# A long-convolution and maxout kernel: the passage from the last frequency pairs to the first feed-forward, with its order, its PSUM banks and its first load changed

## The chip, the cores and the metric

The kernel runs on one core of a Trainium2 chip. The metric is the device time of one execution in microseconds (us); "before" is the median of three runs, and a profile comes from one further execution. Engines are named as in the profile: PE is TensorE's matmul (PEld its weight load), DVE is VectorE, ACT is ScalarE, POOL is GpSimd, SP is SyncE, which only issues DMAs here. Times inside a trace are microseconds from the start of its span.

## The reference: what is computed

Four sequences of 12,544 positions and 128 channels pass a causal long convolution with one learned filter, are multiplied by `x`, and go through a maxout feed-forward with three weight matrices:

```
h = maximum(pos_emb @ w1, 0) @ w2 * exp(-0.01 * pos)        # the filter
u = x * v
y = irfft(rfft(u, 2S) * rfft(h, 2S))[:S];   a = x * y
out = maximum(maximum(a @ moe_w1, a @ moe_w2), a @ moe_w3) @ moe_w_out
```

All of it is float32.

## The kernel before

**The convolution** is a transform of 128 times 90 points with shifted frequencies, split into four stages of matmuls. The first stage turns the 98 samples of each residue into 90 frequencies and keeps them in `spec` (the signal) and `specH` (the filter). The 90 frequencies then go as 45 pairs g (NK = 45) through the second stage (`g_second`, `butterfly`), the product with the filter's spectrum (`g_swap`, `g_re`, `g_im`), the inverse butterfly (`g_unfold`, which makes `ab`) and the third stage (`g_third`, line 649), whose result `zs` is copied by ACT and stored by SP to the DRAM tensor `zd[0]`: one store of two rows for each pair. The fourth stage works on tiles (b, i) of 4 positions times 98 samples: `t_load` (776) reads `zt`, the rows of all 45 pairs for both parts c of a complex number; `t_sums` (799) makes a sum and a difference; `t_last` (815) multiplies by the table `f4p` and then by `x` (`xT`, from `x_load`, 769) into `gt`.

**The feed-forward** uses max(a,b,c) @ wo = max(b-a, c-a, 0) @ wo + a @ wo. `up` (834) makes 128 of the 768 hidden rows: two products into two of the three PSUM banks `hps`, a Relu on ACT (839), a maximum on DVE (842). `down` (845) multiplies by `moe_w_out`. The product `lin` = moe_w1 @ moe_w_out is needed first; it is made by six **folds** (`fold`, 1097): PE transposes 128 columns of moe_w1 (`pt`, 1099), ACT copies them (`w1t`, 1101), PE multiplies them and adds into the bank `pl`. `folding` (1166) lets the multiplication of a fold follow two folds later.

**The order of the work** is written out by hand: every engine executes its own instructions in the order in which the code issues them, and semaphores order the engines among each other. In steps s = 0 to 47 (line 1174) step s issues the second stage of pair s, the filter spectrum of pair s-1 (`s_filter`, into the double bank `h`, copied by ACT to `ht`), the third stage of pair s-3, and the products of pair s-2. The filter spectra are also stored for the later batches (`s_store`, on POOL's queue, ahead of the products). In step 45 two pairs, 43 and 44, are multiplied. Line 1196 says on which engine the addition of `g_im` is done: POOL for 1 < s < 44, DVE otherwise.

Beside these steps the first stage of batch 1 is prepared: `u_load`, `u_mul` (DVE), `u_turn` (a transposition on PE, two copies on ACT) and the **units**, `u_first` (488), which are 32 small matmuls into two banks, a copy on ACT (`high`, 461) and eight operations on DVE: four "sums" (471) and four "fours" (482, 485) that write into `spec`.

After the second stage of pair 44 the order before is: filter 44, third stage 42, unit 0 (step 45); third stage 43, folds 0 to 2 (step 46); third stage 44 (step 47); unit 1, fold 3, turn 4, fold 4, turn 5, fold 5. The order after that is the same in both kernels: units 2, 3 and 4 with their DVE work, the first tile's sums and fourth stage, and the first `up`.

**PSUM.** In this stage the eight banks belong to the pools `cps` (tag `cv`, three banks, used by the second and third stages and by the folds), `sps` (`h`, a double bank, and `pl`) and `gps` (`g`, two banks). A tile asked of a tag takes the next of its buffers and waits until that buffer's last reader is done.

**Queues of DMAs.** SP carries the z stores, the third stage's weights (`load_dir`, 972), `u_load`, and most loads; POOL carries the filter stores and `xT`. For the first tile SP loads `zt` of part 0 and POOL that of part 1; both come after the store of pair 44. The tile (0, 1) is loaded by SP right after it, and (0, 2) in the first `up` (1277), together with its `xT` on POOL.

Of the kernel before, what the change touches and what calls it, by code (L numbers as in the profile page):

```python
# [10 lines left out]
FP32 = mybir.dt.float32  # L11
# [5 lines left out]
P = 128  # L17
# [78 lines left out]
def kernel(  # L96
# [15 lines left out]
    nc = tc.nc  # L112
# [4 lines left out]
    NF = DFF // P  # L117
    NK = N1 // 2
# [9 lines left out]

    zd = [dram.tile([N1, 2, 64, 256] if b == 0 else [N1, 2, 32, 2, 256], FP32, name=f"zd{b}")
          for b in range(B)]  # L130

    f1_t, f1e_t, f1h_t, f4p_t, w_t, wq_t = tables(NB)
    f1_d = nc.inline_tensor(f1_t, name="f1_const").ap()
# [354 lines left out]
    def u_first(*args):  # L488
        for fn in u_products(*args):
            fn()  # L490
# [144 lines left out]
    def g_im(g, apart=False):  # L635
        xt, xs = xts[g], xss.pop(g)
        nc.vector.tensor_tensor(out=xs[:], in0=xs[:], in1=hts.pop(g)[1][:], op=ALU.mult)
        (nc.gpsimd if apart else nc.vector).tensor_tensor(
            out=xt[:], in0=xt[:], in1=xs[:], op=ALU.add)

    def g_unfold(g):
        y = xts.pop(g)
        ab = state["cv"][0].tile([P, 2, 2, D], FP32, tag="ab", name="ab", bufs=2)
        for q, op in enumerate((ALU.add, ALU.subtract)):
            nc.vector.tensor_tensor(out=ab[:, :, q, :], in0=y[:, :, 0, :], in1=y[:, :, 1, :],
                                    op=op)
        abs_[g] = ab

    def g_third(g):
        w, ab = ws.pop((g, 1)), abs_.pop(g)  # L650
        ps = state["cv"][1].tile([P, 512], FP32, tag="cv", name="ps3")
        for k in range(2):
            for q in range(2):
                halves_mm(ps[:, (2 * k + q) * D:(2 * k + q + 1) * D], w[:, k, q, :],
                          ab[:, k, q, :], k == 0 and q == 0, True)
        if g < NK - 2:
            zs = state["cv"][0].tile([P, 2, 256], FP32, tag="z", name="zs", bufs=2)
        else:
            zs = lwp.tile([P, 2, 256], FP32, tag="w1", name="zs")
        nc.scalar.copy(zs[:].rearrange("p k f -> p (k f)"), ps[:])  # L660
        nc.sync.dma_start(
            zd[0][2 * g:2 * g + 2].rearrange("k c t f -> (c t) k f"), zs[:])

# [103 lines left out]
    zts, xTs, gs, pos_, obs = ({} for _ in range(5))  # L767
# [5 lines left out]
                          x[:, 4 * i:4 * i + 8, c, b, :])  # L773
        xTs[b, i], xTs[b, i + 1] = xT[:, 0], xT[:, 1]

    def t_load(b, i, queues=(nc.sync, nc.sync)):
        if b == i == 0:
            x_load(b, i, nc.gpsimd)
        zt = hp.tile([N1, 2, 512], FP32, tag="zt", name="zt", bufs=2)
        for c in range(2):  # L780
            if b == 0:
                queues[c].dma_start(
                    zt[NK * c:NK * c + NK],
                    zd[b].rearrange("(g a) c t f -> g a c t f", a=2)[
                        :, :, c, 2 * i:2 * i + 2, :].rearrange("g a t f -> g a (t f)"))
                continue
            q, j = divmod(i, NT // 2)
            for a in range(2):
                nc.sync.dma_start(
                    zt[NK * c:NK * c + NK, a].rearrange("g (t f) -> g t f", t=2),  # L790
                    zd[b].rearrange("(g a) c t q f -> g a c t q f", a=2)[
                        :, a, c ^ (a & q), 2 * j:2 * j + 2, q, :])
        zts[b, i] = zt[:, 0], zt[:, 1]
        if i % 2 == 0 and (b, i) not in xTs:
            x_load(b, i, nc.gpsimd if 0 < i < NT - 2 and b < B - 1 else nc.sync)

    evens_ = {}
# [282 lines left out]
    cps = pro.enter_context(tc.tile_pool(name="cps0", bufs=3, space=PSUM))  # L1080
    sps = pro.enter_context(tc.tile_pool(name="sps", bufs=1, space=PSUM))
    gps = pro.enter_context(tc.tile_pool(name="gps", bufs=2, space=PSUM))
    def banks_of():
        for pool, tag, n in ((gps, "g", 1), (gps, "g", 1), (sps, "h", 2), (gps, "g", 1),
                             (cps, "cv", 1), (gps, "g", 1)):
            yield pool.tile([P, 512 * n], FP32, tag=tag, name="ps1")[:, 0:512]

    free = banks_of()

    def bank():  # L1090
        return next(free)

    state = {"cv": (cvp, cps), "xb": 2, "bank": bank, "wide": ("ht", 2),
             "turn": lambda: sps.tile([P, 512], FP32, tag="pl", name="pst")}
    Gs, lows = {}, {}

    def fold(f):
        pt = cps.tile([P, 512], FP32, tag="cv", name="pt")
        nc.tensor.transpose(pt[:, 0:D], w_sb[0][:, f * P:(f + 1) * P], eye[:])
        w1t = cvp.tile([P, 2, D], FP32, tag="G", name="w1t", bufs=2)  # L1100
        nc.scalar.copy(w1t[:, 0], pt[:, 0:D])
        return lambda: halves_mm(pl[:, 0:D], w1t[:, 0], wo_sb[:, f, :], f == 0, f == NF - 1)
# [63 lines left out]
    def folding(f):  # L1166
        folded.append(fold(f))
        if len(folded) > 2:
            folded.pop(0)()

    def unit(u):
        u_first(u, (bank(), bank()), "x")

    for s in range(NK + 3):
        if s < NK:
            ws[s, 0] = wf[s]
            s_second(s)
            g_second(s)
            wf.pop(s)
            if s + 3 < NK:  # L1180
                wf[s + 3] = load_dir(s + 3, 0)
        if 1 <= s <= NK:
            g_swap(s - 1)
            s_filter(s - 1)
        if s >= 3:
            ws[s - 3, 1] = wi.pop(s - 3)
            g_third(s - 3)
            if s < NK:
                wi[s] = load_dir(s, 1)
        ready = [g for g in {NK: (s - 2, s - 1)}.get(s, (s - 2,)) if 0 <= g and s <= NK]  # L1190
        for g in {NK - 2: (s - 2, s - 1), NK - 1: (s - 1,), NK: (s - 1,)}.get(s, (s - 2,)):
            if 0 <= g and s <= NK:
                s_store(g)
        for g in ready:
            g_re(g)
            g_im(g, 1 < s < NK - 1)
        if s < NK:
            s_sums(s)
            g_butterfly(s)
        for g in ready:  # L1200
            g_unfold(g)

        if s in muls:
            u_mul(muls[s])
        if s in turns:
            u_turn(turns[s])
        if s in loads:
            u_load(1, loads[s])
        if s == NK:
            unit(0)  # L1210
            pl = sps.tile([P, 512], FP32, tag="pl", name="pl")
        if s == NK + 1:
            for f in range(3):
                folding(f)
    unit(1)
    state["turn"] = bank
    for f in range(3, NF):
        folding(f)
        if f in (3, 4):
            u_turn(f + 1)  # L1220
    while folded:
        folded.pop(0)()
    nc.scalar.copy(lin[:], pl[:, 0:D])
# [5 lines left out]
    f4p = hp.tile([N1, 2, 2, NB // 2], FP32, name="f4p", bufs=1)  # L1229
    nc.sync.dma_start(f4p[:], f4p_d)  # L1230
    sign_t = hp.tile([N1, 1], FP32, name="sign", bufs=1)
    nc.sync.dma_start(sign_t[:], sign_d)
    op_ = ctx.enter_context(tc.tile_pool(name="op", bufs=2))
    conv = ExitStack()
    wp = conv.enter_context(tc.tile_pool(name="wp", bufs=3))
# [19 lines left out]
    for n, (b, i) in enumerate(tiles[:LAST]):  # L1255
        if i == 0:
            plan, pairs_from = plans[b]
        if n == 0:
            t_load(*tiles[0], (nc.sync, nc.gpsimd))
            t_load(*tiles[1])  # L1260
            second_ = u_products(2, (next(hbanks), next(hbanks)))
            second_[0]()
            first_ = ops.tile([D, 512], FP32, tag="ops", name="ps1")
            spare = state["bank"]()
            third = u_products(3)
            fourth = u_products(4, (spare[:, 0:512], spare[:, 512:1024]), "xs")
            t_sums(tiles[0], nc.vector)
            third[0]()
            second_[1]()
            fourth[0]()  # L1270
            t_last(tiles[0], first_)
            second_[2]()
            for fn in fourth[1:]:
                fn()
        for f in range(NF):

            if i < NT - 2:
                if f == 0:
                    t_load(*tiles[n + 2])
            elif i == NT - 1 and f < 2 and n + 1 + f < len(tiles):  # L1280
                t_load(*tiles[n + 1 + f])
            turn_ = i == NT - 1
            if f == 4 and n + 1 == LAST:
                t_sums(tiles[n + 2], nc.vector)
            h = up((b, i), f)
            if n == 0 and f in (1, 2):
                third[f]()
            for a in range(2):
                if f == plan[i][a]:
                    t_sums(tiles[n + 1],  # L1290
                           nc.vector if turn_ or i * NF > pairs_from else nc.gpsimd, (a,))
            late.append(((b, i), f, h))
            if len(late) > 2:
                down(*late.pop(0))
            if f == plan[i][2]:
                t_last(tiles[n + 1])
            if f == 5 and n + 1 == LAST:
                t_last(tiles[n + 2])
            run(besides.pop(n * NF + f, ()))
# [100 lines left out]
```

## Time and the profile before

| | |
|---|---|
| median of 3 runs | 2213.24 us (2212.88 to 2213.73) |
| the profiled execution | 2213.66 us, its span 2211.9 us |
| PE busy | 2192.4 us, 99% of the span |
| DVE, ACT, POOL busy | 69%, 55%, 54% |
| chain that ended last | PE 96%, DMA 1%, DVE 1%, issue 1%, ACT 1% |
| mean granted TensorE clock | 0.997 |
| third stage of pair 44, its copy on ACT ends | 279.1 us, 280.9 us |
| first feed-forward matmul | 292.4 us |

How to read it. A profile counts an engine as busy while one of its instructions runs. "Idle before, releaser" is the time for which the engine had nothing to run before an instruction, and what its wait ended on. The chain of waits goes back from the last instruction, at each step to what released it; so only work that is named there can shorten the time. The view by stretches cuts the span at given times and shows each engine's busy time and the mean granted clock in each.

The passage that the change touches lies between about 255 and 300 us of the span: from the last pairs' products to the first feed-forward.

### The profile page before, as it was taken

To read this page: it belongs to the slowest core of one execution; us is meant where nothing else is said; L and a number is where in the kernel's file an instruction comes from. 1 tells how busy PE (TensorE), PEld (TensorE's weight loads), DVE (VectorE), ACT (ScalarE), POOL (GpSimd) and SP (SyncE) were. 2 spreads that over 40 slices of the span, in tenths; PEclk is the share of its full clock that TensorE was granted. 3 is DMA by queue.
4 is the path that set the end of the run, shared out by engine and by line. 5 is a ranking of instruction groups with operands and counts; after the bars stand their busy time and mean duration, and the time that the engine had idled before them with its cause. 6 is when DMAs were issued, how large, how long until landed. Compare 5 with 4: busy or idle time off the path is not lost.

```text
span 2211.9 us, 77196 instructions
## 1 busy us (share of the span) xinstructions
PE 2192.4 (99%) x31655; PEld 1288.0 (58%) x31655; DVE 1532.6 (69%) x3291; ACT 1211.3 (55%) x2223; POOL 1183.9 (54%) x1579
## 2 busy tenths in 40 slices
PE   9999999999999999999999999999999999999999
PEld 8988755555555455555555555545555545566776
DVE  5588856668888776668888766668878745454443
ACT  3699845456666555456666555556666622222222
POOL 1166567535455566534445566634554426666665
PEclk9999999999999999999999999999999999999999
DMA  8789999889999999779999899879999722222221
GB/s 198 185 267 310 291 181 191 168 192 238 252 247 242 218 188 177 168 178 243 242 247 247 217 196 183 170 162 245 243 242 245 190 77 59 61 71 71 59 59 24
DMA packets 491332, 411.62 MB, mean 186 GB/s; under 512 B 289406, under 2 KB 407920, under 8 KB 490979
## 3 DMA queue, kind: packets, MB, share of 16 engines
q1 hardware_dynamic: 443689, 274.50, 58.1%
q0 software_dynamic: 45808, 130.25, 21.0%
q8 instruction: 249, 4.08, 0.8%
q10 hardware_dynamic: 1482, 1.93, 0.4%
q14 instruction: 104, 0.85, 0.1%
HBM read 262.85 MB, written 84.67 MB: 157 GB/s over the span
## 4 chain that ended last, share of the span: by engine, by line
PE 96%; DMA 1%; DVE 1%; issue 1%; ACT 1%; POOL 0%; SPq 0%; ACTq 0%; DVEq 0%; POOLq 0%
PE hps L167 46%; PE ops L167 20%; PE ops L903 6%; PE cps L167 4%; PE ps L167 4%; PE cps L547 3%; PE cps L449 3%; PE ps L176 3%; PE cps L557 3%; PE sps L1135 2%; PE last L167 1%; PE ps L391 1%; PE gps L1110 1%; PE ps L353 1%; DMA ut<-in_vr_dram 0%
## 5 line engine op out<-in xcount | busy, mean ns | idle before, releaser
L167 PE MATMUL hps<-gt,w_sb 128*64 128x392 f32 (+1 forms) x7672 | 1156.4, 495 | 0.8 <-DVE gt L829 0.7
L839 ACT ACTIVATE hid<-hps 128x392 f32<-128x392 f32 x768 | 382.5, 498 | 749.2 <-PE hps L167 729.7
L167 PEld LDWEIGHTS hps<-gt,w_sb 128*64 128x64 f32 (+1 forms) x7672 | 426.3, 126 | 443.2 <-issue 409.2
L842 DVE TENSOR_TENSOR hid<-hid,hps 128x392 f32<-128x392 f32 x768 | 428.5, 558 | 341.6 <-PE hps L167 323.6
L167 PE MATMUL ops<-hid,wo_sb 128*64 128x392 f32 x2304 | 476.9, 492 | 0.0
L599 POOL TENSOR_TENSOR cb<-cb,xs 128x512 f32<-128x512 f32 x135 | 178.7, 1324 | 358.6 <-DVE xs L596 342.6
L167 PEld LDWEIGHTS ops<-hid,wo_sb 128*64 128x64 f32 x2304 | 165.7, 137 | 213.5 <-issue 213.5
L572 DVE TENSOR_TENSOR cb<-cps,eo 128x512 f32<-128x512 f32 (+1 forms) x288 | 175.2, 650 | 77.2 <-ACT eo L569 74.1
L857 POOL DMA_DIRECT2D out_dram<-ot x96 | 76.7, 799 | 269.6 <-ACT ot L855 250.2
L587 ACT ACTIVATE xs<-cb 32x512 f32<-32x512 f32 x270 | 169.5, 628 | 21.2 <-DVE cb L572 12.3
L588 ACT COPY xs<-cb 32x512 f32<-32x512 f32 x270 | 166.3, 616 | 3.2
L603 DVE TENSOR_TENSOR xs<-cb 128x256 f32<-128x256 f32 x270 | 148.3, 597 | 7.3 <-POOL cb L599 7.3
L429 ACT COPY uT<-turned 113x512 uint16<-113x512 uint16 x180 | 125.9, 770 | 0.0
L580 POOL DMA_DIRECT2D zd<-cb x135 | 94.1, 697 | 39.0 <-DVE cb L572 37.6
L386 POOL TENSOR_TENSOR ut<-ut 128x392 f32<-128x392 f32 x90 | 93.2, 1036 | 36.4 <-DMA ut<-in_vr_dram 34.2
L167 PEld LDWEIGHTS cps<-f4p,even 90*64 90x64 f32 x1552 | 87.2, 138 | 35.9 <-issue 33.3
L772 POOL DMA_DIRECT2D xT<-in_x_dram x172 | 101.8, 610 | 6.7 <-issue 3.3
L471 DVE TENSOR_TENSOR low<-high,cps 128x180 f32<-128x180 f32 x186 | 54.7, 335 | 68.2 <-ACT high L461 68.2
L928 POOL DMA_DIRECT2D out_dram<-o x120 | 72.7, 610 | 46.9 <-DVE o L921 45.5
L167 PE MATMUL cps<-f4p,zt 90*64 90x49 f32 x1552 | 95.8, 222 | 0.0
L413 POOL COPY planes<-ut 128x392 uint16<-128x392 uint16 x180 | 95.5, 566 | 0.0
L167 PE MATMUL cps<-f4p,even 90*64 90x49 f32 x1552 | 94.6, 220 | 0.0
(172 smaller groups left out, 3335.3 us busy)
## 6 DMA issues: line engine op xcount, KB each, us to landing
ht<-hd SPq DMA_DIRECT2D x264, 256.0 KB, 7.1
wt<-wq_const POOLq DMA_DIRECT2D x144, 256.0 KB, 6.1
zd<-cb POOLq DMA_DIRECT2D x135, 256.0 KB, 5.4
zt<-zd SPq DMA_DIRECT2D x384, 90.0 KB, 4.1
sq<-spec SPq DMA_DIRECT2D x528, 64.0 KB, 5.8
ut<-in_xr_dram SPq DMA_DIRECT2D x128, 196.0 KB, 4.2
ut<-in_vr_dram SPq DMA_DIRECT2D x128, 196.0 KB, 4.5
wt<-wt_const SPq DMA_DIRECT2D x90, 256.0 KB, 5.3
```

The lines of the kernel that those rows point to most:

```text
L167: nc.tensor.matmul(out[h:h + w], lhsT[:, h:h + w], rhs, start=start, stop=stop, skip_group_check=True)
L413: nc.gpsimd.tensor_copy(w[:, h, :, :, 0:HB], a[:].bitcast(U16).rearrange("p s (m e h) -> p h s e m", e=2, h=2)[:, h])
L429: nc.scalar.copy(uts[u][0:HR, 8 * (u % 2):8 * (u % 2) + 8].rearrange("n s r t -> n (s r t)").bitcast(U16).rearrange("n (s r t h) -> n h s ...
L572: nc.vector.tensor_tensor(out=cb[:, a, lo:hi], in0=ps[:, lo:hi], in1=eo[:, lo:hi], op=op)
L587: nc.scalar.mul(xs[at:at + 32], xt[at + 32:at + 64], -1.0)
L588: nc.scalar.copy(xs[at + 32:at + 64], xt[at:at + 32])
L599: nc.gpsimd.tensor_tensor(out=xts[g], in0=xts[g], in1=xs[:], op=ALU.add)
L603: nc.vector.tensor_tensor(out=ab[:, q], in0=y[:, 0], in1=y[:, 1], op=(ALU.subtract, ALU.add)[q])
L772: eng.dma_start(xT[c * NG:(c + 1) * NG].rearrange("d i p n -> d (i p) n"), x[:, 4 * i:4 * i + 8, c, b, :])
L839: nc.scalar.activation(h[:], pa[:, 0:N], Relu)
L842: nc.vector.tensor_tensor(out=h[:], in0=h[:], in1=pb[:, 0:N], op=ALU.max)
L903: nc.tensor.matmul(ps[32 * q:32 * q + 32, 0:H2], w[:, m:m + 32], rhs[:, H2 * c:H2 * c + H2], start=start, stop=True, skip_group_check=True)
```

## The change

Six edits; nothing that is computed changes.

1. In step 43 (pair 41) the addition of `g_im` is done on DVE, not on POOL.
2. In step 45 each of the two pairs is unfolded right after its product, so pair 43 ahead of pair 44's product.
3. The steps end at 45, and what follows is written out: unit 0, third stage 43, unit 1, fold 0, third stage 44, folds 1 to 5, with turn 4 after fold 2 and turn 5 after fold 3.
4. PSUM banks: unit 0 takes both `g` banks, unit 1 a `cv` bank and the `h` bank; fold 0 takes a `cv` bank that is held, and folds 1 to 5 go in turn through one more `cv` bank and this one; the turns 4 and 5 take the two `g` banks of unit 0.
5. The rows of the last pair that the first tile needs (2 positions, 2 frequencies, both parts) are also stored in a small DRAM tensor `ze`, part 0 by SP and part 1 by ACT, ahead of the pair's whole store. The first tile is loaded in four DMAs: 44 pairs of each part from `zd[0]` by POOL, the last pair of each part from `ze` by SP.
6. The load of `xT` for tile (0, 2) is issued in the fourth `up` of the first tile, not in the first; the small load `sign` goes from SP to POOL, behind the first tiles' loads.

```
+    ze = dram.tile([2, 2, 2, 256], FP32, name="ze")
...
         nc.scalar.copy(zs[:].rearrange("p k f -> p (k f)"), ps[:])
+        if g == NK - 1:
+            for c in range(2):
+                (nc.scalar if c else nc.sync).dma_start(ze[c], zs[64 * c:64 * c + 2])
         nc.sync.dma_start(
             zd[0][2 * g:2 * g + 2].rearrange("k c t f -> (c t) k f"), zs[:])
...
-    def t_load(b, i, queues=(nc.sync, nc.sync)):
+    def t_load(b, i):
...
             if b == 0:
-                queues[c].dma_start(
-                    zt[NK * c:NK * c + NK],
+                n = NK if i else NK - 1
+                (nc.sync if i else nc.gpsimd).dma_start(
+                    zt[NK * c:NK * c + n],
                     zd[b].rearrange("(g a) c t f -> g a c t f", a=2)[
-                        :, :, c, 2 * i:2 * i + 2, :].rearrange("g a t f -> g a (t f)"))
+                        0:n, :, c, 2 * i:2 * i + 2, :].rearrange("g a t f -> g a (t f)"))
+                if i == 0:
+                    nc.sync.dma_start(
+                        zt[NK * c + n:NK * c + NK].rearrange("o a (t f) -> o a t f", t=2),
+                        ze[c:c + 1].rearrange("o t a f -> o a t f"))
                 continue
...
-        if i % 2 == 0 and (b, i) not in xTs:
+        if i % 2 == 0 and (b or i > 2):
...
     def fold(f):
-        pt = cps.tile([P, 512], FP32, tag="cv", name="pt")
+        pt = next(folds)
...
-    for s in range(NK + 3):
+    for s in range(NK + 1):
...
         for g in ready:
             g_re(g)
-            g_im(g, 1 < s < NK - 1)
+            g_im(g, 1 < s < NK - 2)
+            if s == NK:
+                g_unfold(g)
         if s < NK:
             s_sums(s)
             g_butterfly(s)
-        for g in ready:
-            g_unfold(g)
+            for g in ready:
+                g_unfold(g)
...
+    g0, g1 = one_bank(gps, "g"), one_bank(gps, "g")
+    u_first(0, (g0, g1), "x")
+    ws[NK - 2, 1] = wi.pop(NK - 2)
+    g_third(NK - 2)
+    hb = sps.tile([P, 1024], FP32, tag="h", name="ps1")[:, 0:512]
+    pl = sps.tile([P, 512], FP32, tag="pl", name="pl")
+    u_first(1, (one_bank(cps, "cv"), hb), "x")
+    fb = one_bank(cps, "cv")
+    folds = iter((fb,))
+    folding(0)
+    ws[NK - 1, 1] = wi.pop(NK - 1)
+    g_third(NK - 1)
+    folds = itertools.cycle((one_bank(cps, "cv"), fb))
+    turn_banks = iter((g0, g1))
+    state["turn"] = lambda: next(turn_banks)
+    for f in range(1, NF):
         folding(f)
-        if f in (3, 4):
-            u_turn(f + 1)
+        if f in (2, 3):
+            u_turn(f + 2)
...
-    nc.sync.dma_start(sign_t[:], sign_d)
...
-            t_load(*tiles[0], (nc.sync, nc.gpsimd))
+            t_load(*tiles[0])
             t_load(*tiles[1])
+            nc.gpsimd.dma_start(sign_t[:], sign_d)
...
             turn_ = i == NT - 1
+            if f == 3 and n == 0:
+                x_load(b, 2, nc.gpsimd)
```

More of the change, by code (lines that the diff above doesn't have):

```diff
@@ L1082 @@
     gps = pro.enter_context(tc.tile_pool(name="gps", bufs=2, space=PSUM))
[L1083 to L1093, printed above, removed]
+    state = {"cv": (cvp, cps), "xb": 2, "wide": ("ht", 2),
              "turn": lambda: sps.tile([P, 512], FP32, tag="pl", name="pst")}
@@ L1169, in folding @@
             folded.pop(0)()
-    def unit(u):
-        u_first(u, (bank(), bank()), "x")
-    for s in range(NK + 3):
+    for s in range(NK + 1):
         if s < NK:
@@ L1208, with one_bank @@
             u_load(1, loads[s])
[L1209 to L1217, printed above, removed]
+    def one_bank(pool, tag):
+        return pool.tile([P, 512], FP32, tag=tag, name="ps1")[:]
+    g0, g1 = one_bank(gps, "g"), one_bank(gps, "g")
[14 more added lines that the diff above has]
+    for f in range(1, NF):
         folding(f)
-        if f in (3, 4):
-            u_turn(f + 1)
+        if f in (2, 3):
+            u_turn(f + 2)
     while folded:
```

## The prediction

> **What bounds the kernel now.** The page's first part says TensorE (PE) is busy 99% of the span, so only PE's lost time counts. The list of PE's waits puts nearly all of it in one place: from 258 to 300 us PE waits 8.4 us, and from 300 us to the end 0.5. That stretch is the passage, where the last frequency pairs end and the first feed-forward begins. The chain of waits there (start, us, what) shows two stalls:
>
> ```profile
> 264.46 0.46 POOL hd L1156
> ...
> 265.52 1.28 POOL specH L638
> 266.80 0.02 issue
> 266.83 0.76 DVE ab L645 x2
> ...
> 285.06 4.13 DMA zt<-zd
> ```
>
> First, GpSimd (POOL) does the addition of pair 41 only after the filter store of pair 42, which stands ahead of it and waits for ACT's copy (`ht` L1151, 263.15 to 264.16). Second, the first z load waits for the store of pair 44 (SP's waits name `DMA zd<-zs` for 1.8 us), and its landing releases the sums, whose result `gt` starts at 291.74. VectorE's timeline shows what both cost:
>
> ```profile
> 266.83 0.76 DVE L645 TENSOR_TENSOR ab<-specH 128x256 f32<-128x256 f32 x2 [4.08 <-POOL specH L638]
> 267.50 0.68 DVE L633 TENSOR_TENSOR xt<-xt,ht 128x512 f32<-128x512 f32 x1
> ...
> 277.97 0.59 DVE L482 TENSOR_TENSOR spec<-ps,low 128x180 f32<-128x180 f32 x2
> 278.48 0.59 DVE L485 TENSOR_TENSOR spec<-ps,low 128x180 f32<-128x180 f32 x2
> 281.58 0.60 DVE L471 TENSOR_TENSOR low<-high,ps 128x180 f32<-128x180 f32 x2 [2.52 <-ACT high L461]
> ...
> 289.21 0.69 DVE L808 TENSOR_TENSOR even<-zt 90x512 f32<-90x512 f32 x1 [5.52 <-DMA zt<-zd]
> ```
>
> VectorE idles 4.08 us, then works without a gap from 267.50 to 279.06 (pairs 42, 43, 44, a unit's product, unit 0), then waits again. The third view is busy time by stretch; I cut the stretches where the granted clock changes (stretch, us, PE, PEld, DVE, ACT, POOL, clock, DMA, GB/s):
>
> ```profile
> 262.31:265.72 3.41, 2.06 (x50) 1.57 (x46) 0.44 (x2) 2.75 (x6) 1.24 (x3) 1.00 0.58 189
> 265.72:269.13 3.41, 1.21 (x16) 0.83 (x16) 2.27 (x5) 2.27 (x4) 1.07 (x1) 1.00 0.74 213
> 269.14:272.55 3.41, 2.68 (x40) 2.38 (x42) 3.38 (x10) 2.32 (x5) 1.08 (x2) 0.50 0.55 141
> 275.96:279.37 3.41, 3.35 (x27) 2.40 (x25) 3.07 (x11) 0.93 (x3) 2.18 (x4) 0.50 0.28 65
> 289.62:293.03 3.41, 2.01 (x36) 1.42 (x38) 3.27 (x11) 0.00 (x0) 0.00 (x0) 1.00 0.67 121
> 293.03:296.44 3.41, 3.41 (x14) 1.36 (x14) 3.05 (x11) 0.96 (x2) 2.53 (x2) 0.50 0.78 190
> ```
>
> After 6.8 us with PE 48% busy the clock is 0.50 until 279.4, and it returns after a stretch with PE 98% busy. After 57% (1.90 and 2.01 of 6.82) it is 0.50 once more, as the feed-forward begins.
>
> **Step 1: the addition of pair 41 on VectorE.** It costs 0.69 instead of 1.27 (rows L638) and follows its product, done at 261.06: 261.1 to 261.8. The sums and butterfly of step 43 follow until 262.8 and the unfold until 263.5, so PE has its operand before 265.3, when it has done the filter of pair 43. VectorE then waits for ACT's filter copy of pair 42, which ends at 264.16 as before, and starts pair 42 at 264.2 instead of 267.50. ACT's swap of pair 43 waited for POOL too (266.83); it now follows at 265.1, the filter copy of 43 ends at 267.4, the two of 44 at 269.7 and 270.2, each before VectorE asks for it (267.9, 270.5, 271.1). So the block of 11.56 us runs unbroken from 264.2 to 275.8: 3.3 earlier. Unfold 43 ahead of pair 44 adds nothing to that sum; PE gets third stage 43 at 270.6.
>
> **Step 2: order on PE.** At full clock: filter 44 at 267.4 (ACT must free its bank), third 42, unit 0 to 270.3, third 43 270.6 to 271.7, unit 1 to 272.5, fold 0 to 272.8. Third 44 needs unfold 44, at 275.69 before; unfold 43 now precedes it already, so it ends at 273.15. Its weights are loaded behind pair 41's z store on SP: issued 268.4, plus 4.5 to 4.9 (rows `wt`), 273.3 at the latest. Third 44 runs to 274.3, ACT's copy to 274.95 (280.90 before).
>
> **Step 3: the new wait.** The folds cycle through two held banks. Pool `cv` has three, and the trace shows them taken in turn: fold 2 of before waited 0.46 us for ACT's copy of third 43, three tiles back. Counted so, unit 1, fold 0 and third 44 take the three, and the bank of fold 1 is unit 1's. It is free when VectorE's first pair of "fours" of unit 1 has read it: 275.7 plus 1.72 (276.84 to the end of that row, 278.56) is 277.4. PE idles from 274.3 to 277.5 with folds 1 to 5, both turns, units 2 to 4 and the first fourth stage queued behind.
>
> **Step 4: from fold 1 to the feed-forward.** Folds and turns alternate at 1.50 us as before (280.99 to 282.49). The longest chain is ACT's:
>
> ```profile
> 282.61 1.17 ACT L402 COPY uT<-ps 49x512 f32<-49x512 f32 x2 [0.55 <-PE ps L399]
> 283.80 0.27 ACT L1101 COPY w1t<-pt 128x128 f32<-128x128 f32 x1
> 284.11 1.17 ACT L402 COPY uT<-ps 49x512 f32<-49x512 f32 x2
> 285.30 0.27 ACT L1101 COPY w1t<-pt 128x128 f32<-128x128 f32 x1
> ```
>
> Two fold transposes (0.2 each), a product (0.26) and turn 4 (1.04) from 277.5 end at 279.25; then 1.17+0.27+1.17+0.27+0.27 with small gaps give the last copy at 282.25 to 282.5 against 285.30 to 285.57. The last product ends at 283.0 (286.06), units 2 to 4 at 285.0 (288.10). The fourth stage takes 1.15, so `gt` starts at 286.2 instead of 291.74: **5.54 earlier**.
>
> **Step 5: the load.** POOL issues four x pieces (2.35) after unfold 44 at 273.8, then the two main loads at 276.2 and 276.9; pair 43's store (issued 272.4, plus 2.9 to 3.4) has landed. Landing at 4.13: 281.0. The last rows: store issued at 275.0 on SP and ACT (0.36 to 0.6), landing bounded by 2.0 (the smallest load at the start, 16 KB) and 3.45 (the whole z store); the load behind it again 2.0 to 3.7 (zt on SP). No row shows a transfer of one or two partitions; I take 2.9 and 3.1, the nearest by size and direction: rows in SBUF at 281.0 to 281.8, sums done by 283.3, and with both upper ends by 285.0. PE reaches the fourth stage at 285.0, so 1.7 us of this is slack: **the load is no longer what comes last**. ACT's extra issue (0.6) falls where ACT is idle; without that cover it would cost 0.6. The later x load (2.35 of POOL at f = 3) pushes POOL's planes and sums; the nearest use has 2.8 us and is issued ahead of it, the next have 6.0 (join) and 5.5 (fourth stage of tile 2), and POOL then idles 2.47. Nothing. Uncovered it would cost up to 2.35. The sign load, off SP: nothing, as its use is far away.
>
> **Step 6: the first feed-forward.** Before, at half clock, its third block of eight began 5.00 us after `gt` started: the next group starts at 298.06, less 1.32, is 296.74. At full clock PE would want it after 3.25, but its bank waits for the maximum of block 0, which VectorE ends 4.45 after `gt` starts (296.19). So 0.5 more is gained: 6.04 in all.
>
> **Step 7: the clock.** In the new passage PE is 70% busy in the worst 6.8 us before 272, more than the 67% (282.79 to 289.61) that did not lower it. Across the wait of step 3 it falls to 45%, under the 48% and 57% that did. So I expect 0.50 soon after, between 276.2 and 279.6 depending on where the stretches of 3.41 lie. If it falls after 277.5, the next stretch is full and the clock returns: 3.41 us at about 0.55 of the speed (third stage 1.09 to 1.97) loses 1.5, and ACT's waits in step 4 hide some: 0.9 to 1.5, I take 1.3. The Trainium skill, page "TensorE: Matmul & The Clock Gate", section "Part 1: The HAM clock gate", says that the clock halves after at least one idle window of about 3.4 us and is full again after a busy one. The trace agrees on the stretch, but fell after stretches 36% and 59% busy. By the page the 3.2 us of step 3 would not lower it.
>
> **The sum.** 6.04 - 1.3 = 4.7 us. The profiled execution took 2213.66 (span 2211.9, 1.76 around it): 2209.0. It is 0.42 above the median shown, so 2213.24 - 4.7 = **2208.5**.
>
> **Rivals.**
> - *Two stretches at half clock* (27%): it falls before 277.5, while PE still idles, so the next stretch isn't full; 2.2 to 2.7 lost, 4.5 if the clock takes 10.2 us as at 269.1. For: the three stretches of before; against: a PE with much queued. Gain 3.5: 2209.7, at worst 2211.7.
> - *No half clock* (12%): gain 6.0, 2207.2. Only if a 45% stretch is treated otherwise than those of 48 and 57%. This is what the page's rule gives.
> - *Fold 1 doesn't wait* (8%), the bank being another's: PE goes on at 274.3, waits for unit 0 until 275.8, and the load decides again: sums to 283.3, `gt` 1.12 later at 284.4. Gain 7.8: 2205.4.
> - *The split does nothing* (3%): the main load still waits for the last z store (issued 275.4, landed 278.7, load landed 284.0 to 286.2). `gt` at 286.6 to 288.8: 2207.6 to 2209.8.
> - *Slower* (5%): a transfer of one or two partitions, carried by few engines behind other packets. Two trips in a row cancel everything at 7.3 us each (landing at 289.7), and cost 0.2% from 9.5 each. For: loads took up to 12.3 at the start with ten in flight; against: 2.9 to 4.1 in this passage. At 10 each: 2218.5.
>
> The forecast has 45%. About 0.2% (4.43 us) is what a measurement of this kernel can tell from no change: faster by more are most of the forecast and the second and third rivals, 55%; within it the rest of the forecast, the first and fourth, 40%; slower 5%. The forecast alone spans 2207.9 to 2209.1. The range takes in the second and third rivals and nearly the worst of the first: 2205.4 to 2211.5.
>
> **What would show it.** Right: DVE `ab` of pair 41 near 263 with no wait on POOL; `gt` L829 between 286 and 289; a wait of about 3 us before a fold's transpose L1099 on DVE `spec`; a stretch of clock 0.50 around 277 to 284 and none at 270 or at the first `hps`. Wrong: `gt` released by zt instead of PE; the fold without a wait; PE waiting after 300 us.

## The result and the profile after

The changed kernel took **2205.84 us** (median of 9 runs, 2204.36 to 2209.4) against 2212.87 (9 runs, 2210.95 to 2214.84) of the kernel before, run beside it: a ratio of 0.9971, with a 95% interval of 0.9962 to 0.998. That is 7.0 us, where the forecast had 4.7. The profiled execution took 2205.64, its span 2203.9, mean clock 0.999.

The time was inside the range and the sign was right, but the way was not the forecast's: it came out as the rival in which fold 1 doesn't wait (2205.4). Three rows of PE's list of waits in the passage (us in total, times, longest):

```profile
PE hps L169 <- DVE hid L852: 1.0, 1, 1.0
PE ps L169 <- DMA wt<-wt_const: 1.0, 1, 1.0
PE ps L1099 <- ACT zs L662: 0.7, 1, 0.7
```

The third line is fold 1's transpose. It waits 0.7 us for ACT's copy of third stage 44, not 3 us for DVE: the bank it takes is third stage 44's. DVE's timeline has the other half of the proof: the "fours" that read unit 1's bank last start at 275.21, when fold 1 (273.62) has long begun, so fold 1 can't be in that bank.

```profile
262.33 0.69 DVE L635 TENSOR_TENSOR xt<-xt,ht 128x512 f32<-128x512 f32 x1 [0.57 <-ACT ht L1151]
...
275.21 0.59 DVE L484 TENSOR_TENSOR spec<-ps,low 128x180 f32<-128x180 f32 x2
...
280.76 0.69 DVE L818 TENSOR_TENSOR even<-zt 90x512 f32<-90x512 f32 x1 [4.46 <-DMA zt<-zd]
```

The first of these lines is the start of DVE's block, which began at 267.50 before, behind POOL's addition. It now waits for ACT's filter copy of pair 42, as step 1 has it. That copy ended at 264.16 before and at 262.3 here: this execution reached the passage 1.87 us sooner, most of it gained between 239 and 255 us, ahead of all that the change touches. In the fourteen profiles of this document this copy ends anywhere from 262.30 to 264.25, and in the four that keep pair 41's addition on POOL from 262.67 to 264.16, so the offset is no work of the change. To compare with the profile before, add 1.87 to times of after; this is called the frame of before below.

The chain of waits (start, us, what) has the load in it again:

```profile
270.46 4.16 DMA zd<-zs
...
275.90 4.79 DMA zt<-zd
...
283.30 0.57 DVE gt L839
...
287.80 1.54 PE hps L169 x8
```

The main load of the first tile waits for pair 43's store (4.16), lands after 4.79, and its sums release `gt`. The stretches of the passage (same columns as in the prediction; here two of its eight) show no 0.50:

```profile
268.67:272.08 3.41, 2.41 (x53) 1.83 (x55) 3.27 (x8) 1.81 (x5) 0.59 (x2) 1.00 0.87 270
...
282.32:285.74 3.42, 2.75 (x40) 1.70 (x42) 3.28 (x12) 0.50 (x1) 1.81 (x2) 1.00 0.20 56
```

PE is about 70% busy or more in each of the eight (2.41 of 3.41 us in the first shown, 2.38 in the least busy), and the clock is 1.00 from 5.8 to 2200.6 us, past PE's last matmul (2198.04). Before, it was 0.50 for 10.24 and 3.41 us of the passage.

**Where the time came from.** The third `hps` block starts at 287.80 + 1.87 = 289.67 instead of 296.74: 7.07 us of the passage. Split at two marks: the copy of third stage 44 ends 5.47 earlier (273.57 + 1.87 against 280.90), from there to `gt` takes 9.73 instead of 10.84 (1.11), and from `gt` to the third block 4.50 instead of 5.00 (0.5). The two profiled spans differ by 8.0: the 1.87 ahead of the passage, plus 7.07, less 0.9 that is lost again behind it. About 0.5 of this is lost ahead of PE's last matmul (it ends at 2206.49 before and at 2198.04 here, 8.45 apart) and 0.4 after it; what causes either is open.

### The profile page after: what moved, and what is told of

Read it like the earlier page. It is cut to its first block, busy times and chain, and to the rows that moved or that the text cites. A ratio compares the mean times of both kernels' runs of the same rounds, so it can differ in the third digit from the quotient of the medians.

```text
span 2203.9 us, 77207 instructions
## 1 busy us (share of the span) xinstructions
PE 2186.5 (99%) x31655; PEld 1258.5 (57%) x31655; DVE 1533.7 (70%) x3292; ACT 1211.4 (55%) x2223; POOL 1183.3 (54%) x1580
## 4 chain that ended last, share of the span: by engine, by line
PE 93%; DVE 2%; POOL 2%; issue 1%; DMA 0%; ACT 0%; POOLq 0%; ACTq 0%; DVEq 0%
PE hps L169 46%; PE ops L169 20%; PE ops L913 6%; PE cps L169 4%; PE cps L549 3%; PE cps L451 3%; PE ps L178 3%; PE cps L559 3%; PE ps L169 2%; POOL xt L640 1%; PE last L169 1%; DVE ab L647 1%; PE ps L393 1%; DVE xs L639 1%; POOL specH L640 1%
## 5 line engine op out<-in xcount | busy, mean ns | idle before, releaser
L169 PEld LDWEIGHTS hps<-gt,w_sb 128*64 128x64 f32 (+1 forms) x7672 | 413.7, 126 | 454.5 <-issue 415.9
```

Source lines behind the costliest of these rows:

```text
L169: nc.tensor.matmul(out[h:h + w], lhsT[:, h:h + w], rhs, start=start, stop=stop, skip_group_check=True)
```

## The experiments

Three theories. **A**: the sum above; DVE's early start and the order on PE bring 5.5, the load's path 1.1, the first `up` 0.5. **B**: the order on PE is the gain. **C**: the load's path is the gain. Each gain is the median against that of the kernel before, run beside it (2212.66 for experiments 1 to 4, 2212.96 for 5 to 8, 2213.76 for 9 to 12).

### 1. Edit 1 undone

```
-            g_im(g, 1 < s < NK - 2)
+            g_im(g, 1 < s < NK - 1)
```

> Edit 1 undone alone (pair 41's addition on POOL again, all else as in the changed kernel). Theory A, early VectorE: of the 7.0 us, 3.3 come from VectorE starting pair 42 at once; they are lost here, and PE idles longer around pair 41, so that the clock may fall again: 3.3 to 4.5 us slower than the changed kernel, a gain of 2.5 to 3.7 over before. Theory B, order of PE: the order and the banks carry it, VectorE's start is absorbed by other waits: a gain of 6 or more is left. Theory C, load: the split load carries it: a gain of 6 or more is left. In the trace A expects VectorE idle about 4 us before the unfold of pair 41.

Measured: 2210.36, ratio 0.9989 (0.998 to 0.9998), a gain of 2.3. The chain again has POOL's addition in it, and the load waits behind POOL:

```profile
264.07 1.28 POOL specH L640
...
265.38 0.76 DVE ab L647 x2
...
279.12 5.15 DMA zt<-zd
```

A little under A's range, and far from the 6 or more of B and C: the addition on DVE is worth 4.7 us here, more than the 3.3 by which DVE's block moves. The clock is 0.50 for 6.83 us from 266.9 and for 3.41 from 287.4, which would account for the rest; no run takes the half clock away alone.

### 2. Edit 5 undone: whole store, whole load

```
-                n = NK if i else NK - 1
-                (nc.sync if i else nc.gpsimd).dma_start(
-                    zt[NK * c:NK * c + n],
+                (nc.sync if i or not c else nc.gpsimd).dma_start(
+                    zt[NK * c:NK * c + NK],
...
-                if i == 0:
-                    nc.sync.dma_start(
```

> Edit 5 undone alone (the first tile loaded whole, part 0 by SP and part 1 by POOL, after the store of pair 44; no extra store). Theory A: from the copy of third stage 44 to gt the changed kernel takes 9.7 us, before took 10.8; the whole load gives back 1.1 to 1.6 us, so a gain of 5.4 to 5.9 over before is left. Theory B: the same as A. Theory C, load: the gain falls under 2.

Measured: 2206.25, ratio 0.9973 (0.9963 to 0.9983): a gain of 6.4, 0.6 less than with the split, and within the intervals. C, which wanted under 2, falls; A's 5.4 to 5.9 is missed by half a microsecond, less than the noise. With everything else in place the split is hardly seen:

```profile
277.38 3.81 DMA zt<-zd
...
283.75 0.57 DVE gt L829
```

From the copy to `gt` it takes 10.5 us instead of 9.7. The whole load is issued 1.5 us later than the changed kernel's main load (275.90), but lands after 3.81 instead of 4.79.

### 3. Fold 1 in unit 1's bank: the prediction's step 3, made true

```
-    u_first(1, (one_bank(cps, "cv"), hb), "x")
+    ub = one_bank(cps, "cv")
+    u_first(1, (ub, hb), "x")
...
-    folds = itertools.cycle((one_bank(cps, "cv"), fb))
+    folds = itertools.cycle((ub, fb))
```

> The folds go through the bank of unit 1 and the held one, as the prediction assumed. Fold 1 must then wait until VectorE has read unit 1's bank, at about 275.8 instead of 273.6 in the changed kernel's trace. The prediction's steps 3 and 7: PE idles about 3 us after third stage 44, units 2 to 4 end at 283.3, gt starts at 284.5 instead of 283.3, and the clock falls once for 0.9 to 1.5 more: 1.2 us slower than the changed kernel at full clock, 2.1 to 2.7 with the fall. Theory that the load decides alone: under 0.5 slower.

Measured: 2209.26, ratio 0.9987 (0.9978 to 0.9995), a gain of 3.4. The wait and the stretches:

```profile
PE ps L1099 <- DVE spec L484: 3.1, 1, 3.1
```

```profile
273.14:276.56 3.42, 0.59 (x6) 0.45 (x8) 3.19 (x13) 0.59 (x2) 3.42 (x6) 1.00 0.71 192
276.56:279.97 3.41, 3.41 (x31) 2.83 (x29) 0.00 (x0) 1.66 (x5) 0.09 (x1) 0.50 0.77 199
```

The chain of waits at its end:

```profile
283.70 1.25 PE cps L451 x64
284.95 1.09 PE ps L169 x32
286.07 0.57 DVE gt L839
```

This is the forecast's picture: a wait of 3.1 us (3.2 forecast) on DVE's "fours", one stretch of half clock behind it (the next has 1.00 again), and `gt` at 286.07, released by PE's units and fourth stage and not by the load. In the frame of before (1.84 later, by the copy of pair 42) that is 287.9, where the forecast has 286.2 and the 1.3 of the half clock. The gain is 3.4, the forecast's was 4.7, and by the gains it is 3.6 behind the changed kernel, where 2.1 to 2.7 were expected; the profiled span is 2.5 behind. So steps 3 and 7 work as described once fold 1 has that bank; the changed kernel doesn't have it.

### 4 to 7. One edit alone, one edit or a group undone

Edit 1 alone, on the kernel before:

```
-            g_im(g, 1 < s < NK - 1)
+            g_im(g, 1 < s < NK - 2)
```

> Before with edit 1 alone. Theory A: VectorE's chain 3.3 us earlier, no half clock near 270; third stage 44 ends at about 276 instead of 280.3, gt at 287.6 instead of 291.7: a gain of 4 to 4.6 us. Theory B: under 1.5, since folds 0 to 2 still stand ahead of third stage 44. Theory C: under 1.5, since the load still waits for the last whole store.

Measured: 2210.53, ratio 0.999 (0.9981 to 0.9999), a gain of 2.1 where A wanted 4 or more, and B and C under 1.5. The copy of third stage 44 ends 4.8 us earlier in the span than before, at 276.1, but part of it is given back on the way to `gt` (the 4.40 is the wait for the last whole store, issued at 276.10 and landed at 280.34):

```profile
276.01 4.40 issue
...
281.02 4.23 DMA zt<-zd
...
288.52 0.58 DVE gt L829
```

From the copy to `gt` it takes 12.4 us, 1.6 more than before: 0.9 up to the landing of the load (285.25), and 0.7 in the fourth stage, which runs at half clock (1.76 instead of 1.05). PE ran dry: 1.29 of 3.41 us busy, then clock 0.50 for 6.83.

Edit 5 alone, on the kernel before: `ze`, its store and load, the main loads on POOL (the diff of edit 5 in the section on the change).

> The kernel before with edit 5 alone: last rows in a store and load of their own, main loads on POOL. Theory A (the gain of 7.0 us is 5.5 from third stage 44 and its copy ending earlier, 1.1 from the load path, 0.5 from the first up): in before PE was ready for the fourth stage at 288.1 to 289.3 with its units, and gt started at 291.74 because of the load; so the split alone can win at most 2.4 to 3.6 us less what the late products leave, I expect a gain of 1.5 to 2.9 (about 2210.5). Theory B (the order on PE is what matters): under 1 us. Theory C (the load path is the gain): 5 us or more. In the trace: sums released by zt or ze at about 288 to 289, gt 2 to 3 us earlier against the copy of third stage 44 ... and the same 0.50 stretches of clock around 270.

Measured: 2213.79, ratio 1.0005 (0.9996 to 1.0014). No gain, as B has it (under 1); A, with 1.5 to 2.9, is wrong here too. The chain shows why:

```profile
278.13 2.97 DMA ze<-zs
...
281.97 5.54 DMA zt<-ze
```

A load of a few rows takes 5.54 us, and the whole way from the copy to `gt` 12.8, longer than with the whole load (10.84); 0.7 of that is the fourth stage at half clock, most is the load. What stood beside it is the question of the next two. Edits 1, 5 and 6 without the order, the banks and the unfolding (edits 2, 3, 4):

```
-    u_first(0, (g0, g1), "x")
-    ws[NK - 2, 1] = wi.pop(NK - 2)
-    g_third(NK - 2)
...
-    folding(0)
...
+        if s == NK:
+            unit(0)
...
+        if s == NK + 1:
+            for f in range(3):
+                folding(f)
+    unit(1)
```

> The changed kernel with edits 2, 3 and 4 undone: pair 41's addition on DVE, the split load, the later x load, but unit 0, folds 0 to 2, third stage 44, unit 1, the other folds in the order of before, in its banks. Theory A: DVE's block starts 3.3 us earlier as in the changed kernel, and PE reaches third stage 44 behind three folds and unit 0, about 275.5 in the time of before (2 us later than with the new order); the split takes 1.1 off the wait for the load; gain 3 to 5 us (2208 to 2210), 2 to 4 less than the changed kernel. Theory B (the order is the gain): under 2 us of gain. Theory C (load and DVE, the order does nothing): within 0.7 of the changed kernel. A stretch of clock 0.50 in the wait for the load is to be expected if the order is what kept PE's stretches over 60% busy.

Measured: 2206.87, ratio 0.9974 (0.9963 to 0.9985), a gain of 6.1, above A's 3 to 5 and B's under 2, and close to C's (within 0.7 of the changed kernel). B falls: three small edits do nearly all, and the order, most of the diff, 0.9 by the medians, which the intervals don't tell from nothing. Here the same load lands in 1.87:

```profile
274.97 3.46 DMA ze<-zs
...
279.30 1.87 DMA zt<-ze
```

Against experiment 5 (edit 5 alone) that is 5.54 and 1.87 for the same bytes. The two differ in edits 1 and 6, and edit 6 is the one that moves loads, which the prediction had priced at nothing. The changed kernel with edit 6 undone:

```
-        if i % 2 == 0 and (b or i > 2):
+        if i % 2 == 0 and (b, i) not in xTs:
...
+    nc.sync.dma_start(sign_t[:], sign_d)
...
-            nc.gpsimd.dma_start(sign_t[:], sign_d)
...
-            if f == 3 and n == 0:
-                x_load(b, 2, nc.gpsimd)
```

> The changed kernel with edit 6 undone: xT of tile (0,2) is loaded in the first up again, sign on SP ahead of the z loads. If it costs nothing, as the prediction has it, the time is within 0.4 us of the changed kernel (2205.5 to 2206.2). Rival: POOL's issues of 2.3 us stand ahead of the planes and sums of the first blocks, whose users then wait: 1 to 2 us slower, with a wait of PE or DVE on POOL in the first ten us after gt.

Measured: 2209.81, ratio 0.9985 (0.9976 to 0.9993): a gain of 3.15, 3.9 less than with edit 6. Neither reading of the expectation holds: it is not free, and PE's waits show none for POOL behind `gt`. The cost stands on the chain, on SP and in the DMA:

```profile
276.11 1.04 SPq L1242
...
278.11 6.44 DMA zt<-ze
```

`sign` (L1242) is issued ahead of the loads of the last rows, and the second of these lands after 6.44 us. In this execution the clock also fell at 274.44, for one stretch, behind a wait of 1.7 us for the weights of third stage 44. That is ahead of the first instruction that edit 6 moves (276.11), so the profile alone overstates its cost.

### 8. A bound behind the load: unit 4's DVE work later

In the changed kernel the third block waits 1.0 us for block 0's maximum, which stands behind unit 4's DVE work. Moved behind that maximum:

```
-            for fn in fourth[1:]:
-                fn()
...
+            if n == 0 and f == 0:
+                for fn in fourth[1:]:
+                    fn()
```

> The changed kernel with the DVE work of unit 4 (its later sums and fours) issued behind the first up's maximum rather than ahead of it. The third block of hps starts 4.50 us after gt because its bank waits for the maximum of block 0 on DVE (PE waits 1.0 us for it), and that maximum stands behind unit 4's operations. Theory A (that row is a bound of its own, in series with the load): the maximum of block 0 follows its Relu at once, third block 3.3 to 3.5 us after gt, 1.0 to 1.25 us faster than the changed kernel: about 2204.7. Rival (the wait comes back a few blocks later, when the maxima stand behind the moved operations): no difference, within 0.3 us.

Measured: 2206.45 (2204.65 to 2207.73), ratio 0.997 (0.9958 to 0.9982): not told from the changed kernel. PE's wait for `hid` is gone from the list, as the expectation's theory A has it, but in the profiled execution the last rows came later (`gt` 285.19, 10.3 after the copy), though the program is the changed kernel's up to there; PE ran dry and the first blocks ran at half clock:

```profile
282.59:286.01 3.42, 1.54 (x34) 1.32 (x36) 3.21 (x9) 0.31 (x1) 1.87 (x2) 1.00 0.17 53
286.01:289.42 3.41, 3.41 (x12) 1.21 (x10) 1.51 (x6) 0.50 (x1) 0.67 (x1) 0.50 0.61 166
```

So whether the wait is a bound of its own stays open; no version here beat the changed kernel.

### 9 and 10. The halves of edit 6

Only `sign` back on SP:

```
+    nc.sync.dma_start(sign_t[:], sign_d)
...
-            nc.gpsimd.dma_start(sign_t[:], sign_d)
```

> The changed kernel with one half of edit 6 undone: the small load sign stands on SP again, between f4p and the z loads. With all of edit 6 undone the time was 4.0 us longer, and its profile shows two costs: the issue of sign, 1.04 us of SP ahead of the loads of the last rows, and those loads landing 6.44 us after their issue (4.0 to 4.8 in the changed kernel). Theory S (the queue of SP): 1.0 us slower, up to 2.7 if PE's longer wait lowers the clock for one stretch. Theory X (the x pieces in flight): under 0.5 us slower, SP's z loads being bound by the landing of their store in either case.

Measured: 2208.09, ratio 0.9976 (0.9966 to 0.9985), a gain of 5.7. The difference from the changed kernel, 1.4, is as large as theory S has it, but the intervals overlap, and the chain speaks against its reason: SP spends 2.48 us on `sign`, yet the last rows then land 2.37 us after their issue and `gt` comes 9.8 after the copy, as in the changed kernel (9.7).

```profile
276.81 2.48 SPq L1242
...
280.24 2.37 DMA zt<-ze
...
285.27 0.58 DVE gt L839
```

Only the x load back in the first `up`:

```
-        if i % 2 == 0 and (b or i > 2):
+        if i % 2 == 0 and (b, i) not in xTs:
...
-            if f == 3 and n == 0:
-                x_load(b, 2, nc.gpsimd)
```

> The changed kernel with the other half of edit 6 undone: xT of tile (0,2) is loaded in the first up again, so that POOL issues its four pieces right behind the main z loads; sign stays on POOL. Theory X (the pieces share the DMA engines with the first tile's loads): the last rows land 6 us or more after their issue, gt 1.5 to 2 us later, and with one stretch of clock 0.50 after it 3 to 4 us slower than the changed kernel (2209 to 2210). Theory S: under 1 us slower.

Measured: 2209.48, ratio 0.9983 (0.9974 to 0.9992), a gain of 4.3, 2.7 less than the changed kernel. The chain and the stretches:

```profile
274.81 2.04 DMA ze<-zs
...
277.71 5.87 DMA zt<-ze
...
286.95 0.58 DVE gt L839
```

```profile
280.71:284.12 3.41, 1.56 (x81) 1.38 (x72) 0.41 (x1) 1.38 (x3) 0.00 (x0) 1.00 0.87 150
284.12:287.54 3.42, 2.19 (x32) 1.90 (x32) 2.56 (x8) 0.00 (x0) 1.73 (x2) 0.50 0.10 32
```

X holds, S (under 1 slower) falls. The store of the last rows landed quickly (2.04), then their load took 5.87; POOL had put four x pieces behind its main loads, from 277.74 on, which landed from 283.25 to 284.74. The small load of SP's queue landed at 283.58, in the midst of POOL's pieces. The same load took 5.54 to 6.44 us in the three kernels that have these pieces beside it (experiments 5, 7 and 10). The Trainium skill, page "DMA: Bandwidth & Descriptors", section "Issuing engines are not separate DMA queues", says that DMAs of all issuing engines run on the same 16 DMA engines and interleave; this run agrees, with 5.87 against 1.87 to 4.65 where the pieces are not there.

### 11 and 12. Small edits on the kernel before

Edits 1 and 6 on the kernel before:

```
-            g_im(g, 1 < s < NK - 1)
+            g_im(g, 1 < s < NK - 2)
...
+            if f == 3 and n == 0:
+                x_load(b, 2, nc.gpsimd)
```

> The kernel before with edits 1 and 6 alone: pair 41's addition on DVE, the later x load, sign on POOL; the order, the banks and the whole loads are those of before. Edit 1 alone gained 2.1 us, edits 1, 5 and 6 gained 6.1, and the split (edit 5) was worth 0.4 in the changed kernel. Theory D (edit 6 and edit 1 carry the gain, as the load then lands with no x pieces beside it): 4.5 to 6 us gained, 2207 to 2208.5. Theory E (the split is needed, since the order of before leaves the copy of third stage 44 later): 2 to 3.5 us gained, and PE waits for the load with a stretch of clock 0.50.

Measured: 2210.9, ratio 0.9988 (0.9979 to 0.9996), a gain of 2.9. Theory E holds, D (4.5 to 6) falls: without the split, and with the order of before, the load is too late. PE runs dry twice, the first time although pair 41's addition is on DVE, and after each the clock is 0.50 for 3.41 us:

```profile
267.97:271.39 3.42, 1.56 (x47) 1.21 (x44) 3.35 (x7) 2.18 (x5) 1.05 (x2) 1.00 0.84 246
...
285.04:288.45 3.41, 1.35 (x32) 1.12 (x32) 2.58 (x7) 0.00 (x0) 0.51 (x1) 1.00 0.33 72
```

Edit 6 alone:

```
+            if f == 3 and n == 0:
+                x_load(b, 2, nc.gpsimd)
...
+            nc.gpsimd.dma_start(sign_t[:], sign_d)
```

> The kernel before with edit 6 alone. The load of the first tile landed 4.13 us after its issue in before, with four x pieces issued behind it. Theory D (the x pieces slow it): it lands 0.5 to 1.5 us sooner and the time falls by as much, more if the stretch of clock 0.50 at the first feed-forward (293 to 296 us) goes too, 1 to 2.5 us in all. Theory P (the prediction's: edit 6 does nothing): within 0.4 us of before.

Measured: 2213.29, ratio 0.9996 (0.9987 to 1.0005). Nothing that can be told from noise, as theory P has it: the whole load, which waits for the store, lands after 4.10 us, as before (4.13). So the x pieces, which are beside it before and not here, don't slow this larger load; what experiments 5, 7 and 10 show of the last rows doesn't hold for every load.

### What the twelve say together

The gain, the time at clock 0.50 in the passage of the profiled execution, and the time from the end of the copy of third stage 44 to `gt`:

| kernel | gain, us | at 0.50, us | copy to `gt`, us |
|---|---|---|---|
| all edits | 7.0 | 0 | 9.7 |
| unit 4 later | 6.5 | 3.4 | 10.3 |
| without 5 | 6.4 | 0 | 10.5 |
| 1, 5 and 6 | 6.1 | 0 | 8.9 |
| `sign` on SP | 5.7 | 3.4 | 9.8 |
| x load in the first `up` | 4.3 | 6.8 | 12.2 |
| fold 1 in unit 1's bank | 3.4 | 3.4 | 12.6 |
| without 6 | 3.2 | 6.8 | 12.4 |
| 1 and 6 | 2.9 | 6.8 | 11.8 |
| without 1 | 2.3 | 10.2 | 9.5 |
| 1 alone | 2.1 | 6.8 | 12.4 |
| 6 alone | 0.5 | 13.7 | 11.5 |
| before | 0 | 13.7 | 10.8 |
| 5 alone | -0.8 | 17.1 | 12.8 |

The edits don't add: edits 1, 5 and 6 alone bring 2.1, -0.8 and 0.5, together 6.1. The passage has two places where PE runs dry, the addition of pair 41 and the first load. Edit 1 narrows the first (in experiment 11 half clock still follows it); 5 and 6 together shorten the second, and neither does it alone, because the split rows wait beside the x pieces, and without the split the load waits for the last store. A place left open costs its wait and then, in these profiles, a time at half clock. The first two columns rank the kernels nearly alike, though the half clock is one execution's and the gain a median: the changed kernel and experiment 8 run the same program up to `gt`, and their profiles differ by 3.4 us at 0.50. Edits 2 to 4 matter where another edit is missing: without 5 they raise the gain from 2.9 to 6.4, with all of 1, 5 and 6 there from 6.1 to 7.0. How much of a gain is the wait itself and how much the half clock behind it is argued from the stretches; no run here separates the two. The mean clocks of single runs point to the half clock, but don't settle it: in experiment 4 one run took 2206.74 at a mean clock of 0.999 and the ten others 2209.48 or more at 0.997 or 0.998, yet one run of the changed kernel took 2208.34 at 1.000.

## Why the prediction was right, and where it was not

The range held because it took in the rival of fold 1, to which the prediction gave 8%. The forecast itself was 2.3 us short of the gain (4.7 against 7.0), and its main new cost, the wait of fold 1 with the half clock behind it, did not occur; that the time fell into the range is in part luck.

- **Step 1, right.** DVE's block starts at 262.33 + 1.87 = 264.20, forecast 264.2, released by ACT's filter copy.
- **Step 2, nearly.** The copy of third stage 44 ends at 275.44 in the frame of before, forecast 274.95. Third stage 44 waited 1.0 us for its weights: 5.3 us behind their issue (266.51 to 271.85; 4.5 to 4.9 forecast).
- **Step 3 failed**: "the bank of fold 1 is unit 1's". The view that was trusted, one wait of fold 2 three tiles back, fits a strict turn, but fold 1 got third stage 44's bank, which ACT frees 0.68 us after PE wants it. Experiment 3 gave fold 1 the forecast's bank and had the forecast's wait (3.1) and a gain of 3.4 (4.7 forecast). The assignment of a bank was an inference that no row had tested, and the description of the kernel shares it: a tile does not always take the next buffer in turn.
- **Step 4** follows step 3: with fold 1 at 275.5 in the frame of before instead of 277.5, the last product and the units end 2 us earlier than forecast: units at 281.06 + 1.87 = 282.9 instead of 285.0.
- **Step 5 failed twice.** The rows were forecast in SBUF at 281.0 to 281.8 and were there at 282.6 (280.69 + 1.87, a main load being last), and with the units done at 282.9 "the load is no longer what comes last" is wrong: PE could have begun `t_last` at once, and `gt` would have started 1.15 later, at 282.2 in its own frame, not at 283.30. In experiment 3, where PE is late, `gt` follows PE and not the load. And edit 6 was costed at nothing, since only POOL's own queue was looked at: undone, it costs 3.9 us by the medians, 2.7 with the x pieces alone (experiment 10), where the last rows land after 5.87 us.
- **Step 6, right.** The third block begins 4.50 after `gt`, behind the maximum of block 0 (a wait of 1.0).
- **Step 7** fell with step 3: no long idle time, no half clock. Where the wait was there (experiment 3), the clock fell for exactly one stretch, as forecast: a wait of 3.1 us, with PE 17% busy in its stretch, was enough, against the rival *No half clock*.
- **The sum.** With the terms as measured: 5.5 + 1.1 + 0.5 = 7.1. The rival of fold 1 had 7.8 by the same steps: its `gt` was at 284.4, and came at 283.30 + 1.87 = 285.17, since the load landed 0.8 after the 281.8 it was built on. The forecast's own span, 2207.9 to 2209.1, is wider than its term of 0.9 to 1.5 gives (2208.1 to 2208.7).

## What to carry to other kernels

Where one stall of PE hides behind another, single edits look useless: try them together before throwing one away, and look at the clock of the stretches before the sum. A price of "nothing" for a moved DMA needs two looks, at the issuing queue and at what is in flight on the DMA engines when it starts. And which buffer a pool hands out is read from the wait of the tile that takes it, not from the order of the code: if a forecast turns on it, price both.

## What the runs showed of the hardware

- **The clock.** Over these fourteen profiles the passage had 17 changes from 1.00 to 0.50. In 14 of them PE was busy for 47% or less of the 3.41 us stretch before; in the others 55, 59 and 68%. No stretch of 47% or less was without one, while several of 49 to 60% were. Every return came after a stretch at least 88% busy, and stretches of 57 to 89% at half clock were followed by another. Whether a stretch of 50 to 70% lowers the clock is not settled by these runs.
- **Loads and their neighbours.** The few rows of the last pair took 1.87 us to land in experiment 6 and 6.44 in experiment 7: 5.54 to 6.44 in the three profiles with the x pieces beside them, 1.87 to 4.65 in the six without. The issue of `sign`, a load of 4 bytes a partition, took SP 0.64 us before, 0.40 in experiment 5, 1.04 in experiment 7 and 2.48 in experiment 9, while most of SP's issues in the passage take 0.35 to 1.0.
